# Down projection: the second product of one token pair and the first of the next as one run, the seventh product in a bank of its own

## The chip, the cores and the metric

The kernel runs on one core of one Trainium2 chip. A core has a matrix engine (TensorE, PE in the profile; its weight loads are listed apart as PEld), VectorE (DVE), ScalarE (ACT), GpSimd (POOL) and a queue engine, SyncE (SP), which issues nearly all transfers of this kernel. The engines run side by side and wait for one another by semaphores. Each engine, and SP's queue of transfers too, works in the order in which its instructions were written; what waits holds all that stands behind it. Matrix products are summed in PSUM, eight banks of 128 x 512 float32. The metric is the device time of one execution in microseconds (us); the middle of several executions is compared.

## The reference

One transformer block on 2048 tokens of width 1024: layer norm with scale and shift from a condition, linear attention, a gated residual, a second layer norm, and a gated feed-forward part of width 3584 with its own gated residual.

```python
x = x + ga * _A_ref(h, A_wqkv, A_wo)
h = _layernorm(x, axis=-1) * (1 + cb) + sb
x = x + gb * (_gelu(h @ w_gate) * (h @ w_up) @ w_down)
```

The change touches only the last product, `y @ w_down`, with y of 2048 x 3584, and what follows it: the multiplication by `gb` and the addition of x.

## The kernel before

The down projection takes the tokens in eight pairs of 128-token blocks. For one pair the product is a 2 x 2 block product: two token blocks by two halves of the 3584-wide contraction (even and odd blocks of 128) times two halves of the contraction by two halves of the 1024 output columns. It is done with seven products in place of eight (Strassen's scheme in Winograd's form). Each product is 14 matmuls of 128 x 128 by 128 x 512, one per block index j.

- Products 1 and 2 take y and the weights as they are, in bfloat16 (tiles `ya`, `wd`).
- Products 5, 6, 7, 3 and 4 take sums of y blocks (S0 to S4, tile `sb`, written by `d_s`) and differences of weight blocks (tiles `dt` and `dh`, written by `d_t`), in fp32r, a float32 format. The profile calls them f32.

Product 5 uses S0, 6 uses S1, 7 uses S2, 3 uses S3 and 4 uses S4. S0, S2 and S4 share one buffer and S1 and S3 another, and the two change roles with each pair. So S2 can be written only when product 5 has read S0, and so on. Each sum is two DVE instructions of 896 columns, S4 two ScalarE copies. S0 needs both the even and the odd blocks of the pair.

A pair has four PSUM banks, b0 to b0 + 3; pairs alternate between banks 0 to 3 and 4 to 7. The order before was 1, 5, 6, 2, 7, 3, 4. Product 1 starts bank b0, and ScalarE copies it to bank b0 + 2 (`d_cp`), where products 6, 7 and 4 are added one after another. Product 5 starts bank b0 + 3 and is copied to an SBUF tile `de` (`d_ecp`). `d_add` adds `de` to bank b0 + 2 and writes bank b0 + 1 after product 6, and bank b0 + 3 after product 7. Product 2 is added in bank b0, product 3 in bank b0 + 1. As each of the four output parts is whole, `evac` multiplies it by the gate row (L1576), adds the x part `xq` (L1577) and stores it (L1578). Its DVE instructions stand in the one DVE queue, its store in SP's.

SP's queue carries, for each pair, two loads of y, even and odd blocks (`y_in`, L1571, 896 KB each), four loads of x parts (`x_in`, L1568, 128 KB each) and four stores (L1578). Each `ya` buffer is single: the even blocks of the next pair can be loaded when product 1 and S2 are done with the old ones, the odd blocks when product 2 and S4 are. An `x_in` waits until the store that read the same `xq` buffer has landed. All orders in this part are those of the program text; the planner that reorders an earlier stretch of the kernel does not reach it.

Pair 0 is cut in two: products over the first eight j by the seven-product scheme, the rest by plain products (`down`, L1593), in `d_pair0`. Two of its output parts (1 and 2) are evacuated only during pair 1, by a hook that `d_pair` calls after each product. During pair 1 DVE also makes the last weight differences (`d_t`, L1621). In the last pair DVE multiplies three weight differences by the gate row (`t_gb`, L1652). Product 3 of that pair is cut in two there: eight j with `evac_part` behind them, and after product 4 the other six in a bank of their own, whose sum (`evac_sum`, L1685) is the last DVE work of the kernel.

All products of this part are issued by `d_prod` (L1672).

Of the kernel before, what the change touches and what calls it, by code (L numbers as in the profile page):

```python
# [330 lines left out]
def bass_adaLN_cond__linear_attn_block__geglu_ffn__prompt_kernel(  # L331
# [18 lines left out]
    with ExitStack() as es:  # L350
# [201 lines left out]
        sch = Sched()  # L552
        T, A, V, G, Q = PE_, ACT_, DVE_, POOL_, SP_
# [588 lines left out]
        for c_ in range(10, NCH):  # L1142
            b = seq.index(("k", c_ // 2 * 2, 0)) - (9 if c_ % 2 else 12)
# [422 lines left out]
        def x_in(i, *ns):  # L1566
            for n in ns:
                sch.dma(Q, lambda e, n=n: e.dma_start(XQ[n][:], scr_x[:, 2 * i + n // 2, n % 2 * 512:n % 2 * 512 + 512]), wr=r_xq(n), deps=[x_st[i // 2]], note=f"xq{i}.{n}")  # L1568
# [5 lines left out]
        def evac(c_, k, b, c0, c1):  # L1574
            n = 2 * (c_ % 2) + k
            sch.op(V, lambda e: e.tensor_tensor(PS(b), PS(b), GBB[:, c0:c1], ALU.mult), prd=pr(b), pwr=pr(b), rd=R_GBB, note=f"x2a c{c_}.{k}")  # L1576
            sch.op(V, lambda e: e.tensor_tensor(XQ[n][:, :], PS(b), XQ[n][:, :], ALU.add), prd=pr(b), rd=r_xq(n), wr=r_xq(n), note=f"x2b c{c_}.{k}")  # L1577
            sch.dma(Q, lambda e: e.dma_start(out_v[:, c_, c0:c1], XQ[n][:, :]), rd=r_xq(n), note=f"out{c_}.{k}")  # L1578
# [29 lines left out]
        def d_t(i, q):  # L1608
            j0, j1 = 0, 2
            w = WDT[q][:, 2 * j0:2 * j1, :].rearrange("p (j r) d -> p j r d", r=2)  # L1610
            b = lambda r, cc: (w[:, :, r, cc * 512:(cc + 1) * 512], r_wh(q, r, cc, f"wd{q}", j0, j1))
            t32 = lambda k: (dt_ap(q, k, j0, j1)[0].bitcast(f32), dt_ap(q, k, j0, j1)[1])
            dst, wr = dt_ap(q, i, j0, j1)
            if i == 3:
                src, rd = b(1, 1)
                sch.op(A, lambda e: e.activation(dst, src, ACTF.Copy), rd=rd, wr=wr, note=f"dtcp {q}")
                return
            (in0, r0), (in1, r1) = ((b(0, 1), b(0, 0)), (b(1, 1), t32(0)), (b(1, 1), b(0, 1)), None, (b(1, 0), t32(1)))[i]
            if i == 4:
                in0, in1 = (t_.rearrange("p j (h c) -> p j h c", h=2) for t_ in (in0, in1))  # L1620
            sch.op(V, lambda e: e.tensor_tensor(dst, in0, in1, ALU.subtract), rd=r0 + r1, wr=wr, note=f"dtsum {q}.{i}")  # L1621
# [13 lines left out]
        def d_s(ca, i, hs=(0, 1)):  # L1635
            cb, n = ca + 1, nj(ca)
            for j0, j1 in (((0, min(n, NSJ)), (NSJ, n))[h] for h in hs):
                if j0 >= j1:
                    continue
                dst, wr = ds_ap(ca, i, j0, j1)  # L1640
                if i == 4:
                    src, rd = y_ap(cb, 1, j0, j1)
                    sch.op(A, lambda e, dst=dst, src=src: e.activation(dst, src, ACTF.Copy), rd=rd, wr=wr, note=f"dscp {cb}")  # L1643
                    continue
                s_ = lambda k: (ds_ap(ca, k, j0, j1)[0].bitcast(f32), ds_ap(ca, k, j0, j1)[1])
                (in0, r0), (in1, r1), op = ((y_ap(cb, 0, j0, j1), y_ap(cb, 1, j0, j1), ALU.add), (s_(0), y_ap(ca, 0, j0, j1), ALU.subtract),
                                            (y_ap(ca, 0, j0, j1), y_ap(cb, 0, j0, j1), ALU.subtract), (y_ap(ca, 1, j0, j1), s_(1), ALU.subtract))[i]
                sch.op(V, lambda e, dst=dst, in0=in0, in1=in1, op=op: e.tensor_tensor(dst, in0, in1, op), rd=r0 + r1, wr=wr, note=f"dssum{i} {cb}")  # L1648

        def t_gb(q):  # L1650
            t_, r_ = dt_ap(q, 3, 0, 2)
            sch.op(V, lambda e: e.tensor_tensor(t_, t_.bitcast(f32), GBB[:, 512:1024].unsqueeze(1).to_broadcast([P, 2, 512]), ALU.mult), rd=r_ + R_GBB, wr=r_,  # L1652
                   note=f"dtsum gb{q}")

        def d_prod(ca, b0, k, own=None, js=None):
            b = b0 + {1: 0, 2: 0, 5: 3, 6: 2, 7: 2, 4: 2, 3: 1}[k] if own is None else own
            i = {1: None, 2: None, 5: 0, 6: 1, 7: 2, 3: 3, 4: 4}[k]
            o = None
            js = range(nj(ca)) if js is None else js
            for j in js:  # L1660
                q, jj = divmod(j, 2)
                dst = PS(b)
                if i is None:
                    l_, rl = y_ap(ca, k - 1, j, j + 1)
                    r_, rr = WDT[q][:, 2 * jj + k - 1, 0:512], r_wh(q, k - 1, 0, f"wd{q}", jj, jj + 1)
                else:
                    l_, rl = ds_ap(ca, i, j, j + 1)
                    t_, rr = dt_ap(q, i, jj, jj + 1)
                    r_ = t_[:, 0]
                    if i == 4:  # L1670
                        dst = dst.rearrange("p (h c) -> p h c", h=2)
                o = sch.op(T, lambda e, l_=l_, r_=r_, j=j, dst=dst: e.matmul(dst, l_[:, 0, :], r_, start=(k in (1, 5) or own is not None) and j == js[0], stop=j == js[-1], skip_group_check=True),  # L1672
                           rd=rl + rr, pwr=(pr(b) if j == js[0] else ()), note=f"down P{k} c{ca} j{j}", overwrite_ok=True)
            pset_writer(b, o)

# [15 lines left out]
        def d_cp(dst, src, note):  # L1691
            sch.op(A, lambda e: e.activation(PS(dst), PS(src), ACTF.Copy), prd=pr(src), pwr=pr(dst), note=note)

        def d_add(dst, src):
            sch.op(V, lambda e: e.tensor_tensor(PS(dst), PS(src), DE[:, :], ALU.add), prd=pr(src), rd=R_DE, pwr=pr(dst), note="dpadd")

        def d_ecp(b):
            sch.op(A, lambda e: e.activation(DE[:, :], PS(b), ACTF.Copy), prd=pr(b), wr=R_DE, note="descp")
# [5 lines left out]
        def d_pair0(hook):  # L1704
            parts = parts_of(0)
            for k in (2, 6, 5, 0, 7, 3, 13, 11, 12, 4):
# [12 lines left out]
                    d_add(3, 2)  # L1719
                hook(k)  # L1720

        def d_pair(i, hook):
            ca, b0 = 2 * i, i % 2 * 4
            last = i == 2 * CPG - 1
            parts = parts_of(i)

            def y_next(r):
                if not last:
                    y_in(i + 1, r)

            for k in (1, 5, 6, 2, 7, 3, 4):
                if last and k == 3:
                    d_prod(ca, b0, 3, None, range(6, NDJ))
                    evac_part(*parts[1])
                    continue
                d_prod(ca, b0, k)
                if k == 1:
                    d_cp(b0 + 2, b0, "dpcp")
                elif k == 5:
                    d_ecp(b0 + 3)  # L1740
                    d_s(ca, 2)
                elif k == 6:
                    d_add(b0 + 1, b0 + 2)
                    d_s(ca, 3)
                    y_next(0)
                elif k == 2:
                    evac(*parts[0])
                elif k == 7:
                    d_add(b0 + 3, b0 + 2)
                    d_s(ca, 4)  # L1750
                    y_next(1)
                    evac(*parts[3])
                elif k == 3:
                    evac(*parts[1])
                    d_s(ca + 2, 0)
                else:
                    if not last:
                        d_s(ca + 2, 1)
                    evac(*parts[2])
                    if last:  # L1760
                        d_prod(ca, b0, 3, 0, range(6))
                        evac_sum(*parts[1][:2], 0, *parts[1][3:])
                hook(k)
# [62 lines left out]
        for n in range(12):  # L1826
            q, i = divmod(n, 4)
# [56 lines left out]
        def hooks(i):  # L1884
            def hook(k):
                more = i + 1 < 2 * CPG
                if i == 1:
                    if k == 1:
                        d_t(2, 5)
                        d_t(2, 6)  # L1890
                    if k in (6, 2, 7):
                        d_t(4, {6: 4, 2: 5, 7: 6}[k])
                    if k in (6, 7):
                        n = 1 if k == 6 else 2
                        evac(*parts_of(0)[n])
                        x_in(1, n)
                else:
                    if k == 1:
                        x_in(i, 0, 3, 1)
                    elif k == 5:  # L1900
                        x_in(i, 2)
                    if not more and k in (5, 6):
                        for q in {5: (0, 1), 6: (2,)}[k]:
                            t_gb(q)
            return hook

        d_pair0(hook0)
        for i in range(1, 2 * CPG):
            d_pair(i, hooks(i))

# [74 lines left out]
```

## Time and profile before

| | us |
|---|---|
| three runs | 782.47, 782.76, 783.43 |
| median | 782.76 |
| span of the profiled execution (first to last instruction) | 780.9 |
| PE / DVE / ACT busy in the span | 770.2 / 645.9 / 374.6 |
| down projection, first to last matmul | 598.6 to 778.0 |
| granted TensorE clock, whole span | 1.00 |

The profile is one execution. Its own device time is not recorded beside the span; the median of the runs is 1.9 above the span, which is what lies before the first and behind the last instruction. A row of the timeline shows the start, the length, the engine and line, what is written and read, how many like instructions were merged into the row, and in brackets how long the engine had been idle and what ended that. "SPq" rows are SP issuing transfers; their length is that of issuing, not of the transfer. Merged SP rows include the waits between the issues. When the text says that a load landed so many us after its issue, the landing is the one that the trace holds for that transfer.

### The profile page before, as it was taken

The page shows a single profiled execution, that of the slowest core. Times are in us where ns is not written, and L with a number is a line of the kernel's source. Part 1 is how long each engine was busy: PE and PEld are TensorE (multiplying, and loading weights), DVE is VectorE, ACT ScalarE, POOL GpSimd, SP SyncE. Part 2 cuts the span into 40 slices and gives each one's busy share as a digit, 9 for nine tenths or more (in the row PEclk, how much of TensorE's full clock was granted, in tenths as well). Part 3 has the DMA queues.
Part 4 walks back from the last instruction along what each step waited for, and adds up shares of the span by engine and source line. Part 5 has one row for each costly group of instructions (what it writes and reads, how often), then busy time and mean ns, then how long its engine had stood idle before and what let it go on. Part 6 is the DMA issues. An engine that isn't in the chain of part 4 may idle for free.

```text
span 780.9 us, 10753 instructions
## 1 busy us (share of the span) xinstructions
PE 770.2 (99%) x3825; PEld 496.2 (64%) x3883; DVE 645.9 (83%) x964; ACT 374.6 (48%) x629; POOL 47.5 (6%) x126
## 2 busy tenths in 40 slices
PE   8999999999999999999999999999999999999998
PEld 4444445666445667667676767667676576677766
DVE  6699988897899878787989888888989888676767
ACT  2497743242466487878755555555555211111111
POOL 2031300000321011100000000000000000000000
PEclk9999999999999999999999999999999999999999
DMA  9879749939999358867353865535356334443331
GB/s 284 256 167 252 158 91 215 255 80 196 203 287 231 82 138 212 230 175 215 99 145 108 250 211 172 148 96 161 97 147 221 111 127 139 144 141 114 126 125 60
DMA packets 196940, 130.22 MB, mean 167 GB/s; under 512 B 69516, under 2 KB 182420, under 8 KB 195864
## 3 DMA queue, kind: packets, MB, share of 16 engines
q1 hardware_dynamic: 196872, 129.55, 62.4%
q8 instruction: 30, 0.49, 0.3%
q14 instruction: 22, 0.18, 0.1%
q10 hardware_dynamic: 16, 0.00, 0.0%
HBM read 92.55 MB, written 23.35 MB: 148 GB/s over the span
## 4 chain that ended last, share of the span: by engine, by line
PE 95%; SPq 2%; DMA 1%; DVE 1%; issue 1%; ACT 0%; DVEq 0%; ACTq 0%
PE ps_all L1458 45%; PE ps_all L1672 21%; PE ps_all L895 7%; PE ps_all L934 7%; PE ps_all L1283 7%; PE ps_all L880 5%; PE ps_all L1593 1%; SPq L598 1%; DMA wmq<-in_w_mod_dram 1%; SPq L603 1%; DMA h1T<-xh 0%; PE ps_all L913 0%; PE ps_all L1201 0%; PE ps_all L1240 0%; DVE h1T L724 0%
## 5 line engine op out<-in xcount | busy, mean ns | idle before, releaser
L1458 PE MATMUL ps_all<-ss,tp 128*128 128x512 f32 x896 | 214.3, 396 | 0.0
L1458 PEld LDWEIGHTS ps_all<-ss,tp 128*128 128x128 f32 x896 | 168.3, 188 | 37.8 <-DVE ss L1413 0.2
L1672 PE MATMUL ps_all<-dt,sb 128*128 128x512 f32 x424 | 102.5, 398 | 0.0
L1481 ACT ACTIVATE ge<-ps_all 128x512 f32<-128x512 f32 x112 | 64.1, 597 | 73.8 <-DVE ps_all L1469 62.1
L1458 PE MATMUL ps_all<-h2a,wt 128*128 128x512 bf16 x421 | 95.7, 379 | 1.8
L1672 PEld LDWEIGHTS ps_all<-dt,sb 128*128 128x128 f32 x424 | 79.6, 188 | 18.5 <-DVE sb L1648 0.3
L1476 DVE TENSOR_TENSOR ps_all<-ps_all,es 128x512 f32<-128x512 f32 x54 | 37.6, 699 | 49.4 <-ACT es L1466 49.0
L1488 DVE TENSOR_TENSOR ys<-ge,ps_all 128x512 bf16<-128x512 f32 x112 | 74.4, 684 | 3.8 <-PE ps_all L1672 0.5
L1458 PEld LDWEIGHTS ps_all<-h2a,wt 128*128 128x128 bf16 x448 | 38.0, 98 | 57.3 <-ACT ps_all L1463 16.9
L1433 DVE TENSOR_TENSOR tp<-wt 128x1024 fp32r<-128x1024 bf16 x56 | 68.1, 1217 | 1.8 <-DMA wt<-in_B_w_up_dram 1.8
L1433 DVE TENSOR_TENSOR tp<-wt,tp 128x1024 fp32r<-128x1024 bf16 x56 | 68.2, 1218 | 0.0
L934 PE MATMUL ps_all<-h1T,wq 128*128 128x512 bf16 x256 | 56.7, 379 | 0.0
L880 PE MATMUL ps_all<-wk,h1T 128*128 128x512 bf16 x239 | 55.3, 379 | 1.1 <-DMA wk<-in_A_wqkv_dram 0.5
L1283 PE MATMUL ps_all<-w,pq 128*128 128x512 bf16 x249 | 55.7, 379 | 0.5 <-issue 0.2
L1458 PE MATMUL ps_all<-ar,tp 128*128 128x512 f32 x224 | 55.5, 390 | 0.0
L869 ACT ACTIVATE eb<-ps_all 128x512 f32<-128x512 f32 x64 | 36.3, 594 | 37.6 <-PE ps_all L880 16.0
L1672 PE MATMUL ps_all<-wd,ya 128*128 128x512 bf16 x199 | 47.5, 380 | 0.7
L1458 PEld LDWEIGHTS ps_all<-ar,tp 128*128 128x128 f32 x224 | 42.1, 188 | 8.9
L1463 ACT ACTIVATE ps_all<-ps_all 128x512 f32<-128x512 f32 x56 | 32.6, 582 | 26.8 <-PE ps_all L1458 26.5
L934 PEld LDWEIGHTS ps_all<-h1T,wq 128*128 128x128 bf16 x256 | 25.0, 98 | 30.0
L1283 PEld LDWEIGHTS ps_all<-w,pq 128*128 128x128 bf16 x256 | 24.6, 98 | 30.3 <-issue 1.1
L1643 ACT ACTIVATE sb<-ya 128x896 fp32r<-128x896 bf16 (+1 forms) x16 | 14.5, 913 | 58.8 <-PE ps_all L1672 58.8
(141 smaller groups left out, 976.3 us busy)
## 6 DMA issues: line engine op xcount, KB each, us to landing
wt<-in_B_w_gate_dram SPq DMA_DIRECT2D x28, 512.0 KB, 4.0
wt<-in_B_w_up_dram SPq DMA_DIRECT2D x28, 512.0 KB, 5.2
scr_y<-ys SPq DMA_DIRECT2D x28, 512.0 KB, 3.2
ya<-scr_y SPq DMA_DIRECT2D x14, 896.0 KB, 4.9
rb<-scr_rd SPq DMA_DIRECT2D x32, 256.0 KB, 6.0
wd<-in_B_w_down_dram SPq DMA_DIRECT2D x7, 1024.0 KB, 7.6
wmst<-in_w_mod_dram SPq DMA_DIRECT2D x6, 1024.0 KB, 6.2
wmq<-in_w_mod_dram SPq DMA_DIRECT2D x8, 512.0 KB, 7.5
```

The costliest lines, as they stand in the source:

```text
L869: sch.op(A, lambda e: e.activation(EB[i][:, :], PS(bank), ACTF.Exp), prd=pr(bank), wr=rng, note=f"{note}.exp")
L880: o = sch.op(T, lambda e, dc=dc: e.matmul(PS(bank), H1[sg][:, ci, dc, :], W_[:, dc, jg * 512:(jg + 1) * 512], start=(dc == 0), stop=(dc == ...
L895: o = sch.op(T, lambda e, c_=c_: e.matmul(PS(bank, 0, n), PK[c_][:, g * P:(g + 1) * P], xrow(c_, o_, o_ + n), start=(c_ == 0), stop=(c_ == ...
L934: o = sch.op(T, lambda e, dc=dc: e.matmul(PS(b), WQ[:, dc, qc * P:(qc + 1) * P], H1[sg][:, :, dc, :], start=(dc == 0), stop=(dc == NDC - 1 ...
L1283: last[half] = sch.op(T, lambda e, g=g, half=half: e.matmul(PS(b0 + half), PQ[sg][:, g, ci * P:(ci + 1) * P], W2[:, g, half * 512:(half + ...
L1433: sch.op(V, lambda e: e.tensor_tensor(TP[k][:], in0, in1 if k in (0, 2) else in1[:], ALU.subtract), rd=r0 + r1, wr=r_tp(k), deps=[x1_ops[7 ...
L1458: o = sch.op(T, lambda e, l_=l_, r_=r_, dc=dc: e.matmul(PS(b), l_, r_, start=fresh and dc == 0, stop=dc == ND2 - 1, skip_group_check=True) ...
L1463: sch.op(A, lambda e: e.activation(PS(BB + t), PS(BA + t), ACTF.Copy), prd=pr(BA + t), pwr=pr(BB + t), note="pcp")
L1476: sch.op(V, lambda e: e.tensor_tensor(PS(BC + t), PS(BC + t), ES[t][:, :], ALU.add), prd=pr(BC + t), rd=r_2k(OFF_ES[t], f"es{t}"), pwr=pr( ...
L1481: sch.op(A, lambda e: e.activation(GE[i][:, :], PS(b), ACTF.Gelu_apprx_tanh), prd=pr(b), wr=r_2k(OFF_GE[i], f"ge{i}"), note="gelu")
L1488: sch.op(V, lambda e: e.tensor_tensor(YS[s_][:, 2 * h:2 * h + 2, t, :], q(GE[i][:, :]), q(PS(b + 1)), ALU.mult), rd=r_2k(OFF_GE[i], f"ge{i ...
L1672: o = sch.op(T, lambda e, l_=l_, r_=r_, j=j, dst=dst: e.matmul(dst, l_[:, 0, :], r_, start=(k in (1, 5) or own is not None) and j == js[0] ...
```

## The change

The order of the products in a pair becomes 5, 6, 7, 2, then product 1 of the next pair, then 3 and 4. Product 1 of pair 1 is issued ahead, behind pair 0. So product 2 of one pair and product 1 of the next stand next to one another, both in bfloat16.

Product 7 no longer adds to bank b0 + 2. For pairs 1 to 7 it starts bank b0 + 3, which product 5 has left by then. A new function `d_join` has ScalarE copy it to `de`, and DVE adds `de` to bank b0 + 1 (result to bank b0 + 3) and to bank b0 + 2. Pair 0 keeps its form.

What stood behind the moved products moves along: the load of the next pair's odd blocks (`y_next(1)`) from behind product 7 to behind product 2, and the evacuation of part 3 stays behind product 7. The hooks are spread anew. In pair 1 the weight differences and the evacuation of pair 0's part 2 stand behind products 6, 7 and 2. The x loads of a pair stand behind product 1 (part 3) and product 4 (part 0) of the pair before, and behind its own product 5 (parts 1 and 2). The three scalings of the last pair stand behind products 7 (two) and 2 (one), where they stood behind 5 and 6.

```diff
-            b = b0 + {1: 0, 2: 0, 5: 3, 6: 2, 7: 2, 4: 2, 3: 1}[k] if own is None else own
+            b = b0 + {1: 0, 2: 0, 5: 3, 6: 2, 7: 3 if ca else 2, 4: 2, 3: 1}[k] if own is None else own
...
-start=(k in (1, 5) or own is not None) and j == js[0]
+start=(k in (1, 5) or k == 7 and ca > 0 or own is not None) and j == js[0]
...
+        def d_join(b0):
+            d_ecp(b0 + 3)
+            d_add(b0 + 3, b0 + 1)
+            d_add(b0 + 2, b0 + 2)
+
+        def d_open(i):
+            b = i % 2 * 4
+            d_prod(2 * i, b, 1)
+            d_cp(b + 2, b, "dpcp")
...
-            for k in (1, 5, 6, 2, 7, 3, 4):
+            for k in (5, 6, 7, 2, 1, 3, 4):
+                if last and k == 1:
+                    continue
...
+                if k == 1:
+                    d_open(i + 1)
+                    hook(k)
+                    continue
                 d_prod(ca, b0, k)
-                if k == 1:
-                    d_cp(b0 + 2, b0, "dpcp")
-                elif k == 5:
+                if k == 5:
                     d_ecp(b0 + 3)
                     d_s(ca, 2)
                 elif k == 6:
                     d_add(b0 + 1, b0 + 2)
                     d_s(ca, 3)
                     y_next(0)
+                elif k == 7:
+                    d_join(b0)
+                    d_s(ca, 4)
+                    evac(*parts[3])
                 elif k == 2:
+                    y_next(1)
                     evac(*parts[0])
-                elif k == 7:
-                    d_add(b0 + 3, b0 + 2)
-                    d_s(ca, 4)
-                    y_next(1)
-                    evac(*parts[3])
...
                 if i == 1:
-                    if k == 1:
-                        d_t(2, 5)
-                        d_t(2, 6)
-                    if k in (6, 2, 7):
-                        d_t(4, {6: 4, 2: 5, 7: 6}[k])
+                    if k in (6, 7, 2):
+                        d_t(4, {6: 4, 7: 5, 2: 6}[k])
                     if k in (6, 7):
                         n = 1 if k == 6 else 2
                         evac(*parts_of(0)[n])
                         x_in(1, n)
                 else:
-                    if k == 1:
-                        x_in(i, 0, 3, 1)
-                    elif k == 5:
-                        x_in(i, 2)
-                    if not more and k in (5, 6):
-                        for q in {5: (0, 1), 6: (2,)}[k]:
+                    if k == 5:
+                        x_in(i, 1, 2)
+                    if not more and k in (7, 2):
+                        for q in {7: (0, 1), 2: (2,)}[k]:
                             t_gb(q)
+                if more and k in (1, 4):
+                    x_in(i + 1, 3 if k == 1 else 0)
...
         d_pair0(hook0)
+        d_open(1)
+        d_t(2, 5)
+        d_t(2, 6)
         for i in range(1, 2 * CPG):
             d_pair(i, hooks(i))
```

More of the change, by code (lines that the diff above doesn't have):

```diff
@@ L1671, in d_prod @@
                         dst = dst.rearrange("p (h c) -> p h c", h=2)
-                o = sch.op(T, lambda e, l_=l_, r_=r_, j=j, dst=dst: e.matmul(dst, l_[:, 0, :], r_, start=(k in (1, 5) or own is not None) and j == js[0], stop=j == js[-1], skip_group_check=True),
+                o = sch.op(T, lambda e, l_=l_, r_=r_, j=j, dst=dst: e.matmul(dst, l_[:, 0, :], r_, start=(k in (1, 5) or k == 7 and ca > 0 or own is not None) and j == js[0], stop=j == js[-1], skip_group_check=True),
                            rd=rl + rr, pwr=(pr(b) if j == js[0] else ()), note=f"down P{k} c{ca} j{j}", overwrite_ok=True)
```

## The prediction

> **What bounds the kernel now.** I read the page's busy line and its chain of work first. The chain says which engine sets the end.
>
> ```profile
> PE 770.2 (99%) x3825; PEld 496.2 (64%) x3883; DVE 645.9 (83%) x964; ACT 374.6 (48%) x629; POOL 47.5 (6%) x126
> ...
> PE 95%; SPq 2%; DMA 1%; DVE 1%; issue 1%; ACT 0%; DVEq 0%; ACTq 0%
> ```
>
> TensorE (PE) is busy nearly everywhere and is 95% of the chain. So an edit pays only if it shortens PE's own stream, and costs only if it makes PE wait or lengthens what follows its last matmul. The change touches the down projection alone, so I read the timeline of one steady pair there (start, length, both in us).
>
> ```profile
> 686.65 0.70 DVE L1576 TENSOR_TENSOR ps_all<-ps_all,gbb 128x512 f32<-128x512 f32 x1 [0.94 <-PE ps_all L1672]
> ...
> 689.49 2.09 DVE L1648 TENSOR_TENSOR sb<-ya,ya 128x896 fp32r<-128x896 bf16 x2 [1.34 <-DMA ya<-scr_y]
> 689.62 2.71 PEld L1672 LDWEIGHTS ps_all<-wd,ya 128*128 128x128 bf16 x14 [0.26 <-issue]
> ...
> 692.44 6.35 PEld L1672 LDWEIGHTS ps_all<-dt,sb 128*128 128x128 f32 x28
> ...
> 711.66 2.71 PEld L1672 LDWEIGHTS ps_all<-wd,ya 128*128 128x128 bf16 x14 [0.26 <-issue]
> ```
>
> Two pairs' first products start 711.66 - 689.62 = 22.04 apart. The f32 loads step by (6.35 - 0.19) / 27 = 0.228; longer undisturbed runs give 0.2267. The bf16 matmuls step by 0.216. Without any seam a pair is 70 x 0.2267 + 28 x 0.216 = 21.92, so the two bf16 runs cost 0.12 together: **0.06 per run**. The 0.26 of idle printed at each run's start is the weight loader's, and most of it lies under matmuls that still stream.
>
> Third, the stretch where the first two pairs overlap, since DVE is fullest there (18.1 of the 20 us from 640 to 660), with SyncE's (SP's) queue.
>
> ```profile
> 640.17 0.32 SPq L1568 DMA_DIRECT2D xq<-scr_x  x1
> 640.54 0.43 SPq L1578 DMA_DIRECT2D out_dram<-xq  x1
> ...
> 641.08 0.36 SPq L1571 DMA_DIRECT2D ya<-scr_y  x1
> ...
> 643.06 2.92 SPq L1578 DMA_DIRECT2D out_dram<-xq  x2
> ...
> 647.06 2.09 DVE L1648 TENSOR_TENSOR sb<-ya,ya 128x896 fp32r<-128x896 bf16 x2
> 647.77 0.33 SPq L1568 DMA_DIRECT2D xq<-scr_x  x1
> ...
> 648.36 1.79 PEld L1672 LDWEIGHTS ps_all<-dt,sb 128*128 128x128 f32 x8
> ```
>
> The load at 641.08 brings the odd blocks of pair 2. The sum S0 made from it starts at 647.06, and pair 2's fifth product, its first user, at 648.36: there is only 0.2 to spare once S0's first half (1.09) is made. The xq load at 647.77 is issued behind an output (the second of the two from 643.06, at 645.65) whose landing it waits for, 2.1 later. Such a wait holds all of SP's queue.
>
> Last, the end.
>
> ```profile
> 776.20 1.32 PEld L1672 LDWEIGHTS ps_all<-dt,sb 128*128 128x128 f32 x6
> ...
> 776.62 0.70 DVE L1576 TENSOR_TENSOR ps_all<-ps_all,gbb 128x512 f32<-128x512 f32 x1 [1.36 <-PE ps_all L1672]
> 777.43 0.69 DVE L1577 TENSOR_TENSOR xq<-ps_all,xq 128x512 bf16<-128x512 f32 x1
> 778.03 0.68 DVE L1685 TENSOR_TENSOR xq<-ps_all,de 128x512 bf16<-128x512 f32 x1
> 778.74 0.33 SPq L1686 DMA_DIRECT2D out_dram<-xq  x1
> ```
>
> DVE idles 1.36 before the last three operations: it keeps up with PE, and the last sum starts 1.83 after the last six loads do.
>
> **The change part by part.** *Fewer bf16 runs.* Pairs 1 to 7 have two each, 14. After it there are 8: one for pair 1's first product, six merged, one second product in the last pair. Six fewer by 0.06 is **-0.4**. Matmul counts do not change. By the printed idle it would be 6 x 0.26 = 1.6; I take 0.4, since the pair's pitch already contains all that a run costs.
>
> *Seventh product in its own bank.* Per pair this adds a ScalarE copy (0.60, the row of the fifth product's copy) and one DVE add (0.61 pitch, 0.70 long). In a steady pair, counted from its fifth product's start, the seventh ends near 10.0, the copy at 10.6, the adds at 11.9, the evacuation of part 3 at 13.4 and of part 0 at 14.8. DVE then idles until the third product ends at 19.2. Bank 1 is wanted by the third product only at 15.6, and bank 2 by the fourth at 18.8. So this costs nothing, hidden by DVE's idle time; without that cover it would be at most 0.6 a pair.
>
> *S0 of the next pair.* The fifth product now follows the fourth directly. After the third product's end at 19.24: evacuation 1.42, first half 1.09, done at 21.8; the fifth starts at 21.98. It just fits. S2, wanted by the seventh at 6.35, has its first half by 5.2. The range here is 0 to 0.1 a pair; I take 0.
>
> *The even-block load, steady.* The next pair's first product moves up to 12.56. Its load stands in SP behind part 2's output (issued near 4.2), two xq loads and a third that waits for that output's landing (1.7 to 2.1), so it is issued near 6.7. The full ya loads of this stage whose landing the trace holds took 4.5 to 6.05 from issue (over all 18 ya loads the median is 4.8, the longest 7.3): it lands at 11.2 to 12.75. I take nothing; the upper end is 0.25 in each of six pairs, 1.5.
>
> *The odd-block load of pair 2.* This is the costly step. It moves from behind the seventh product to behind the second, which in pair 1 puts it past the output of pair 0's part 2 and the xq load that waits for that output's landing. DVE after the evacuation of pair 0's part 1 (its last row starts at 637.68, 0.6 to the next): from 638.28 two adds 1.21, part 3 of pair 1 1.41, one weight difference 1.13, pair 0's part 2 1.49, to 643.5. Output issued at 643.6, xq load 1.8 to 2.1 behind it (both gaps stand in SP's rows: 638.39 to 640.17, 645.65 to 647.77), the ya load 0.4 later, near 645.9; landing 4.8 later, 650.7; S0's first half 0.1 + 1.09 with 0.05 to PE: 651.9. PE without the wait would be there at 648.3. So PE waits **3.6**, by the ends (4.5 after the shorter gap, 6.05 after the longer) 3.2 to 5.1. Behind this wait on DVE stand S0's second half, S1 and part 2's evacuation; S1 is ready at 654 against its product's start at 655, so nothing more is late. The wait occurs once: from pair 2 on no foreign output stands before that load, it leaves near 13.9 and lands by 18.8 (20 with the slowest landing), against 20.6.
>
> *The tail.* The last pair's three scalings of weight differences by the gate row (1.22 each, pitch 1.135) move from behind the fifth and sixth products to behind the seventh and second. DVE from the copy's end at 10.7: adds 1.21, part 3 1.40, two scalings 2.27, part 0 1.40, the third 1.135, the partial evacuation 1.39, part 2 1.40: the last sum starts at 20.9. The last six matmuls' loads start at 17.6, so the sum starts 3.3 after them instead of 1.83: **+1.45**, between 1.2 and 1.7 by the spread of pitches. The third scaling ends at 18.2, its first user starts at 18.5: no wait there.
>
> *Sum:* -0.4 + 3.6 + 1.45 = **+4.65**. The profiled execution's span of 780.9 becomes 785.6. The median of 782.76 stands 1.9 above that span (launch and end around it, taken as unchanged): **787.4**, 0.6% slower.
>
> [...] The trace's longest PE idle is 2.2 us, at the very start, and the granted clock reads 1.00 in every window. A wait of 3.6 has no row. [...] I sum at full clock.
>
> **The rivals.**
> *The clock drops in the wait.* [...] For it: the idle is longer than any in the trace. Against: the clock of 1.00 after 2.2 idle. Chance 0.10.
>
> *Every pair waits for its even blocks.* If those loads take 6.05, as the four behind xq loads at 655, 675, 697 did or nearly did, six waits of 0.25 come on top: 788.9. Against: only one xq load is fresh before them now. Chance 0.10.
>
> *The odd-block load is not late.* If the change doesn't hold it back (its landing by 647), only runs and tail remain: 782.76 - 0.4 + 1.45 = 783.8, within 0.2%. Against: SP's rows issue strictly in order and show that very wait. Chance 0.07.
>
> *The other side: a seam costs far more than the pitch says.* Place: the six removed runs. To end over 0.2% faster (1.57) against 3.6 + 1.45, each must be worth over 1.1. The pitch gives 0.06, the printed idle 0.26, so only a cost in the rows' blind spots could do it, for instance 1.2 each: 780.6. Chance 0.03.
>
> **How the numbers follow.** My forecast has 0.70, with 786.8 to 789.2 as its own range (3.2 + 1.2 - 0.4 to 5.1 + 1.7 - 0.4 on 782.76). The overall range is 785.6 to 789.8: its lower end is the forecast's lower end with 0.26 instead of 0.06 for each of the six runs, its upper end takes in most of the two dearer rivals, and what is left out are the two cheap rivals and about 0.07 above. A change of 0.2% (1.6 us) is about what a measurement of this kernel can tell from none. Slower: 0.70 + 0.10 + 0.10 = 0.90; within: 0.07; faster: 0.03.
>
> **What would show it.** In the profile after: the fifth product of pair 2 waits over 3 us for DVE's S0, which waits for a ya load issued near 646, behind an xq load; eight bf16 starts with 0.26 of loader idle, six of them 28 loads long; pairs about 21.98 apart; DVE without idle from the last seventh product to the last sum, which starts over 3 behind the last six loads; a granted clock of 1.00 around 652. I am wrong if the ya load of pair 2 is issued by 642, if the six middle pairs grow above 22.04, or if the last sum still starts within 2 of the last loads.

## The result and the profile after

The changed kernel takes 789.35 us (median of five executions; 788.86 to 790.96) against 782.76 before. The ratio is 1.0089, with a 95% interval of 1.0077 to 1.0100: 0.9% slower. The profiled execution took 790.67; its span is 788.9, 8.0 above the 780.9 of before.

First the page: the chain of work by engine, and the row of the granted TensorE clock over 40 slices.

```profile
PEclk9999999999999999999999999999999998999999
...
PE 93%; DMA 3%; DVE 2%; SPq 2%; issue 0%; DVEq 0%; ACT 0%; ACTq 0%
```

PE has 93% of the chain instead of 95, and transfers and DVE have gained. One slice of the clock row, from about 651 to 671, has an 8. The view of waits names what PE waited for, total, times and longest:

```profile
PE ps_all L1672 <- DVE sb L1648: 3.4, 1, 3.4
...
PE ps_all L1672 <- DMA ya<-scr_y: 0.3, 1, 0.3
```

Both are new, and both are in the down projection. The timeline where pairs 1 and 2 meet shows the first, SP's queue ahead of the rest:

```profile
641.16 2.92 SPq L1578 DMA_DIRECT2D out_dram<-xq  x2
645.48 0.33 SPq L1568 DMA_DIRECT2D xq<-scr_x  x1
645.92 0.37 SPq L1571 DMA_DIRECT2D ya<-scr_y  x1
...
645.34 3.13 PEld L1672 LDWEIGHTS ps_all<-dh,sb 128*128 128x128 f32 x14
...
646.92 0.69 DVE L1577 TENSOR_TENSOR xq<-ps_all,xq 128x512 bf16<-128x512 f32 x1
651.16 2.09 DVE L1648 TENSOR_TENSOR sb<-ya,ya 128x896 fp32r<-128x896 bf16 x2 [3.55 <-DMA ya<-scr_y]
...
652.31 9.70 PEld L1672 LDWEIGHTS ps_all<-dt,sb 128*128 128x128 f32 x32 [3.84 <-DVE sb L1648]
```

The load of pair 2's odd blocks is issued at 645.92 (641.08 before), behind the x load at 645.48, which waited for the landing of the second store in the row above (issued at 643.75). It lands at 651.07. DVE idles 3.55, makes S0, and the fifth product starts at 652.31. Its predecessor's 14 loads started at 645.34, so it was due 14 x 0.2267 later, at 648.51: PE lost **3.8**.

The windows (busy time and number of instructions of each engine, then granted clock, transfer share and GB/s) show what the wait set off:

```profile
648.00:650.00 2.00, 0.90 (x4) 0.39 (x3) 0.00 (x0) 0.00 (x0) 0.00 (x0) 1.00 0.92 346
650.00:652.00 2.00, 0.00 (x0) 0.00 (x0) 0.83 (x1) 0.00 (x0) 0.00 (x0) 0.74 0.60 210
652.00:654.00 2.00, 1.69 (x4) 1.40 (x5) 2.00 (x3) 0.00 (x0) 0.00 (x0) 0.50 0.00 0
...
656.00:658.00 2.00, 2.00 (x7) 1.58 (x6) 1.66 (x2) 0.00 (x0) 0.00 (x0) 0.55 0.18 61
658.00:660.00 2.00, 2.00 (x10) 1.61 (x9) 1.09 (x1) 0.60 (x1) 0.00 (x0) 1.00 0.65 178
```

The clock is halved from about 650.96 (0.74 over 2 us is half speed for 1.04) to 657.8, 6.8 us. Six or seven f32 matmuls fall in 2 us there, ten after it: by their starts they step by 0.427 instead of 0.227. Twelve of them do, which is **2.4** more.

The steady pairs are as short as forecast, by the loads:

```profile
686.51 5.73 PEld L1672 LDWEIGHTS ps_all<-wd,ya 128*128 128x128 bf16 x28 [0.26 <-issue]
692.35 3.17 PEld L1672 LDWEIGHTS ps_all<-dt,sb 128*128 128x128 f32 x14
...
708.48 3.57 PEld L1672 LDWEIGHTS ps_all<-wd,ya 128*128 128x128 bf16 x18 [0.26 <-issue]
```

One bf16 run of 28 loads per pair, and 708.48 - 686.51 = 21.97 per pair, 0.067 less than before. One pair is longer:

```profile
724.94 0.34 SPq L1578 DMA_DIRECT2D out_dram<-xq  x1
725.37 3.84 SPq L1568 DMA_DIRECT2D xq<-scr_x  x3
...
729.31 0.37 SPq L1571 DMA_DIRECT2D ya<-scr_y  x1
730.45 2.70 PEld L1672 LDWEIGHTS ps_all<-wd,ya 128*128 128x128 bf16 x14 [0.26 <-issue]
...
733.91 2.70 PEld L1672 LDWEIGHTS ps_all<-wd,ya 128*128 128x128 bf16 x14 [0.75 <-DMA ya<-scr_y]
```

The store at 724.94 took 3.9 to land, the third x load waited for it and held the even-block load until 729.31. The first product of the next pair, due 14 x 0.216 behind 730.45, came 0.43 late. Last the tail:

```profile
782.68 1.32 PEld L1672 LDWEIGHTS ps_all<-dt,sb 128*128 128x128 f32 x6
...
784.55 0.69 DVE L1576 TENSOR_TENSOR ps_all<-ps_all,gbb 128x512 f32<-128x512 f32 x1
785.34 0.69 DVE L1577 TENSOR_TENSOR xq<-ps_all,xq 128x512 bf16<-128x512 f32 x1
785.95 0.68 DVE L1685 TENSOR_TENSOR xq<-ps_all,de 128x512 bf16<-128x512 f32 x1
```

DVE has no idle left (1.36 before), and the last sum starts 3.27 behind the last six loads, where it was 1.83.

| where the 8.0 of the profiled execution lie | us |
|---|---|
| the down projection begins later (598.73 for 598.56, ahead of all that changed) | +0.2 |
| wait of pair 2's fifth product | +3.8 |
| half clock behind it | +2.4 |
| wait for even blocks near 733 | +0.4 |
| tail | +1.4 |
| six bf16 runs fewer | -0.4 |
| sum | +7.8 |

### The profile page after: what moved, and what is told of

Same layout as the page of the kernel before. It is cut to its first block, busy times and chain, and to the rows that moved or that the text cites. A ratio compares the mean times of both kernels' runs of the same rounds, so it can differ in the third digit from the quotient of the medians.

```text
span 788.9 us, 10827 instructions
## 1 busy us (share of the span) xinstructions
PE 776.8 (98%) x3883; PEld 498.4 (63%) x3883; DVE 648.1 (82%) x971; ACT 377.0 (48%) x636; POOL 47.4 (6%) x126
## 4 chain that ended last, share of the span: by engine, by line
PE 93%; DMA 3%; DVE 2%; SPq 2%; issue 0%; DVEq 0%; ACT 0%; ACTq 0%
PE ps_all L1458 45%; PE ps_all L1672 18%; PE ps_all L895 7%; PE ps_all L1283 7%; PE ps_all L934 7%; PE ps_all L880 6%; PE ps_all L1593 1%; DMA ya<-scr_y 1%; DMA wmq<-in_w_mod_dram 1%; SPq L598 1%; SPq L603 1%; PE ps_all L913 0%; DVE xq L1577 0%; DVE dt L1652 0%; DVE ps_all L1576 0%; DVE ps_all L1695 0%
## 5 line engine op out<-in xcount | busy, mean ns | idle before, releaser
L1458 PE MATMUL ps_all<-h2a,wt 128*128 128x512 bf16 x448 | 101.6, 380 | 0.0
L1672 PEld LDWEIGHTS ps_all<-dt,sb 128*128 128x128 f32 x424 | 81.4, 192 | 22.2 <-DVE sb L1648 4.1
L1698 ACT ACTIVATE de<-ps_all 128x512 f32<-128x512 f32 x15 | 9.0, 597 | 103.6 <-PE ps_all L1672 103.6
```

The source lines that it names most:

```text
L1458: o = sch.op(T, lambda e, l_=l_, r_=r_, dc=dc: e.matmul(PS(b), l_, r_, start=fresh and dc == 0, stop=dc == ND2 - 1, skip_group_check=True) ...
```

## The experiments

My theory was that one load, held back in SP's queue, causes the wait in pair 2, that this wait halves the clock, and that the scalings cause the tail. The rivals were DVE's own load in pair 1, a clock that falls for another reason, and a price of the added copy and add in every pair. In the first four runs the kernel before had 782.68, in the last four 782.87.

### Pair 0's part 2 behind product 2

```diff
-                    if k in (6, 7):
+                    if k in (6, 2):
                         n = 1 if k == 6 else 2
                         evac(*parts_of(0)[n])
                         x_in(1, n)
```

> The changed kernel, with the evacuation of pair 0's part 2 and the x load that waits for its store moved from behind product 7 to behind product 2 of pair 1, so that the load of pair 2's odd blocks no longer stands behind them. Nothing is left out. Theory (queue order makes that load late): it is issued near 641.6 instead of 645.9 and lands by 647; the wait of pair 2's fifth product falls from 3.8 us to 0.2 or less, the granted clock stays 1.00, and 3.6 plus the 0.6 to 2.4 of half-clock time go: 783 to 785. Rival (the wait comes from DVE's load in pair 1, not from the queue): the wait stays above 2 us, since DVE does the same work in that stretch.

Measured: 784.25 (783.54 to 785.5), 1.0020 of before (1.0011 to 1.0030). The timeline:

```profile
641.16 0.36 SPq L1571 DMA_DIRECT2D ya<-scr_y  x1
...
648.21 3.97 PEld L1672 LDWEIGHTS ps_all<-dt,sb 128*128 128x128 f32 x18 [0.19 <-DVE sb L1648]
```

The load is issued 4.8 earlier (the whole stretch lies 0.4 earlier in this trace), and the loader's idle before the fifth product falls from 3.84 to 0.19. DVE does the same work in that stretch, so its load was not the cause. The granted clock is between 0.998 and 1.00 in all ten executions, against 0.995 to 0.997 in the changed kernel's five. About 5 of the 6.6 are gone by moving two DVE instructions and two transfers. What is left of the loss, 1.6, is about the tail, which this run leaves as it was.

### Only the x load moved

```diff
                     if k in (6, 7):
                         n = 1 if k == 6 else 2
                         evac(*parts_of(0)[n])
-                        x_in(1, n)
+                    if k in (6, 2):
+                        x_in(1, 1 if k == 6 else 2)
```

> The changed kernel, with only the x load of pair 1's part 2 moved behind product 2; the store of pair 0's part 2 stays ahead of the load of pair 2's odd blocks. Theory: the load is issued near 644.1 (1.8 earlier, the landing of the store that the x load waited for), lands near 649, and the fifth product waits 1.5 to 2.0 instead of 3.8. By the clock theory, an idle of PE below 2 us leaves the granted clock at 1.00: 784.9 to 786. Rival (any wait here drops the clock): the clock falls below 1.00 behind this wait as well, and the time is 1 to 2.5 higher.

Measured: 785.44 (784.95 to 787.11). The timeline:

```profile
643.15 0.38 SPq L1571 DMA_DIRECT2D ya<-scr_y  x1
...
649.47 2.61 PEld L1672 LDWEIGHTS ps_all<-dt,sb 128*128 128x128 f32 x12 [2.02 <-DVE sb L1648]
```

The wait is 2.0 in place of 3.8 (the load is issued 2.8 earlier, but the whole stretch lies 1.0 earlier in this trace): the part of it that the x load's wait for a landing had caused is gone, the part that the store ahead caused is left. In five of six executions the clock stays at 0.999 or 1.00; in the profiled one (0.999) PE itself idled 1.6. The slowest, 787.11, shows 0.997 and has no trace. So the theory's forecast for the clock held in five of six.

### The wait filled with matmuls

```diff
+                if i == 1 and k == 4:
+                    d_fill(14, 3)
```

`d_fill(n, b)` issues n matmuls of `wd` by `wd` into bank b.

> The changed kernel, with 14 plain bf16 matmuls of no use (about 3.0 us) put between the fourth product of pair 1 and the fifth of pair 2, in a bank that the fifth product starts anew. They fill the wait and change no load, no DVE work and no queue of transfers. Theory (the clock fell because PE idled): S0 comes at the same moment as in the changed kernel and the fifth product starts as late, but the granted clock stays 1.00 and its matmuls step by 0.23, so the time is 787 to 788.4, with less spread than 788.9 to 791.0. Rival (the clock falls for another reason, such as the load that lands then): matmuls behind it step by 0.43 still, 789 to 791.

Measured: 787.67 (787.28 to 789.3), clock 0.999 or 1.00 in all four. Timeline and windows:

```profile
652.41 3.73 PEld L1672 LDWEIGHTS ps_all<-dt,sb 128*128 128x128 f32 x17 [0.82 <-DVE sb L1648]
```

```profile
653.00:655.00 2.00, 2.00 (x10) 1.67 (x9) 2.00 (x3) 0.00 (x0) 0.00 (x0) 1.00 0.00 0
```

The fifth product starts at 652.41 as against 652.31, so the late load is untouched. But ten matmuls fall in 2 us behind it where the changed kernel had six or seven. So it was PE's idling that halved the clock (3.4 in the changed kernel, 0.3 here): the loads, DVE's work and the queues were the same. The forecast of less spread did not hold (2.0 against 2.1). The execution of 789.3 is the profiled one: there the even-block load of pair 3 took 7.45 to land (issued 659.06), and PE waited for it 1.3.

### The scalings earlier

```diff
-                    if not more and k in (7, 2):
-                        for q in {7: (0, 1), 2: (2,)}[k]:
-                            t_gb(q)
+                    if not more and k in (5, 6, 2):
+                        t_gb({5: 0, 6: 1, 2: 2}[k])
```

> The changed kernel, with the three scalings of the last pair's weight differences behind products 5, 6 and 2 (one each) instead of 7, 7 and 2. Theory (they lengthen the tail by standing on DVE between the last seventh product and the last sum): the last sum starts 1.85 to 1.95 behind the loads of the last six matmuls instead of 3.27, and the time falls by 1.35 to 787.5 to 789.6 (the wait in pair 2 and the clock's spread stay). Rival (the tail is set by the last stores or by the other added DVE work): the distance stays above 2.8 and the time does not move.

Measured: 788.80 (787.3 to 790.63). The tail in the timeline:

```profile
782.01 1.32 PEld L1672 LDWEIGHTS ps_all<-dt,sb 128*128 128x128 f32 x6
...
782.43 0.70 DVE L1576 TENSOR_TENSOR ps_all<-ps_all,gbb 128x512 f32<-128x512 f32 x1 [0.46 <-PE ps_all L1672]
...
783.85 0.68 DVE L1685 TENSOR_TENSOR xq<-ps_all,de 128x512 bf16<-128x512 f32 x1
```

The last sum starts 1.84 behind the last loads, as before the change, and DVE waits for PE again. So the tail of 1.43 is the scalings' place. The median fell by 0.55 only, where 1.35 was forecast. The half clock behind pair 2's wait is still there (0.996 or 0.997), and the four executions spread by 3.3, so the time alone could not have shown the tail's share. What spreads them is not shown: 788.57 and 790.63 have the same clock of 0.996.

### Fewer matmuls in the wait

```diff
-                    d_fill(14, 3)
+                    d_fill(4, 3)
```

> The changed kernel with 4 useless bf16 matmuls (0.9 us) in the wait of pair 2 instead of 14, so that PE idles about 2.5 to 2.8. Theory (the clock falls by how much PE did in fixed stretches of 3.41 us, since both half-clock times seen lasted 6.83 = 2 x 3.41): it falls in some executions and not in others, by where the wait lies in the stretch; times of 787.3 to 790.5, granted clock from 0.995 to 1.00. Rival (only an idle of 3.41 or more lets it fall): the clock stays at 0.999 or 1.00 in every execution, 787.3 to 788.3.

Measured: 788.40. The four executions, time and granted clock: 786.73 and 788.02 at 0.999, 788.78 and 789.33 at 0.997. One of them lies below the range of the theory. The profiled one is that of 788.02:

```profile
652.63 1.46 PEld L1672 LDWEIGHTS ps_all<-dt,sb 128*128 128x128 f32 x7 [2.98 <-DVE sb L1648]
```

PE itself idled 2.5 there, and the clock stayed at 1.00 in the windows over the wait. In two others the granted clock is lower, but they have no trace, so how long PE idled in them is not known.

The traces at hand tell more of the theory. In the profile of the changed kernel the time from one change of the clock to the next is 189 times 3.413 us at full clock, 2 times at half and 38 times at full; in that of the kernel before it is 227 times at full clock. The last change is a fall behind the last matmul, where it costs nothing. Steps of 3.413 counted back from it give stretches for the other traces too; that the clock could have changed only at their borders is the author's estimate from these counts. Here is PE's busy time (the second number) in the stretches that hold the wait: two of the changed kernel, one of this run, one of the run that moved only the x load.

```profile
647.55:650.96 3.41, 1.35 (x6) 0.77 (x5) 0.06 (x1) 0.00 (x0) 0.00 (x0) 1.00 0.89 320
650.96:654.37 3.41, 2.06 (x5) 1.68 (x6) 3.21 (x4) 0.00 (x0) 0.00 (x0) 0.50 0.09 31
...
648.33:651.75 3.42, 1.82 (x9) 0.75 (x7) 0.26 (x1) 0.00 (x0) 0.00 (x0) 1.00 0.91 338
...
648.05:651.46 3.41, 1.99 (x9) 1.65 (x10) 3.14 (x4) 0.00 (x0) 0.00 (x0) 1.00 0.22 75
```

The clock fell at the end of the stretch with PE busy for 1.35, and not behind those with 1.82 and 1.99. The run with earlier scalings fell behind 1.33. At the kernel's end it fell behind 1.29 (in the first run of the next section) and not behind 1.86 (in the run with pair 0's part 2 moved). In the changed kernel the stretch with 2.06 of busy time at half clock was followed by another at half clock, and that one, with PE busy for all of its 3.42, by full clock. The border counted so cuts this run's idle of 2.5 into 1.6 and 0.9, and the clock fell behind neither part. The rival, which asks for an idle of 3.41, is refuted by the changed kernel's own trace, where the clock fell 2.1 into the idle, and by the run with earlier scalings, where the whole idle was 3.33. The ends of matmuls are modelled in a profile, so the busy times are rough.

### All three mended

```diff
-                    if k in (6, 7):
+                    if k in (6, 2):
                         n = 1 if k == 6 else 2
                         evac(*parts_of(0)[n])
                         x_in(1, n)
...
-                    if k == 5:
+                    if k == 6:
                         x_in(i, 1, 2)
...
-                    if not more and k in (7, 2):
-                        for q in {7: (0, 1), 2: (2,)}[k]:
-                            t_gb(q)
+                    if not more and k in (5, 6, 2):
+                        t_gb({5: 0, 6: 1, 2: 2}[k])
```

> The changed kernel with three moves and nothing left out: pair 0's part 2 and its x load behind product 2 of pair 1; the three scalings behind products 5, 6 and 2; the x loads of a pair's parts 1 and 2 behind product 6, after the load of the next pair's even blocks. Theory (all of the loss is late loads, the half-clock time that the largest of them causes, and the scalings): pair 2's fifth product waits 0.3 at most, no first product waits for its even blocks, the last sum starts under 2 behind the last loads, and what remains is the gain of six runs of 0.06: 782.1 to 783.0 against about 782.7 before. Rival (the added copy and add for the seventh product, or the order itself, cost something in every pair): pairs are longer than 22.04 and the time stays above 783.5.

Measured: 782.63 (782.10 to 783.15), 0.9996 of before (0.9987 to 1.0005). A second version adds further moves in the order of DVE and SP:

```diff
             elif k == 12:
                 ...
                 evac(*parts_of(0)[3])
+                evac(*parts_of(0)[1])
+                x_in(1, 1)
...
-                    if k in (6, 2):
-                        n = 1 if k == 6 else 2
-                        evac(*parts_of(0)[n])
-                        x_in(1, n)
+                    if k == 6:
+                        evac(*parts_of(0)[2])
+                        x_in(1, 2)
...
                 elif k == 7:
                     d_join(b0)
                     d_s(ca, 4)
-                    evac(*parts[3])
                 elif k == 2:
                     y_next(1)
+                    evac(*parts[3])
                     evac(*parts[0])
```

> As the run before, with three more moves: pair 0's part 1 is evacuated before pair 1 starts, its part 2 behind product 6, and the evacuation of part 3 of every pair stands behind product 2, after the load of the odd blocks, so that this load is issued at product 2's end (near 639.5 for pair 2 instead of 641.2). Theory: also the last 0.3 of wait in pair 2 goes; pairs of 21.97 throughout: 781.9 to 782.6, by 0.0 to 0.1% faster than before. Rival (late evacuation of part 3 holds up the fifth product or DVE): waits of PE for DVE appear in every pair, above 783.

Measured: 782.35 (781.74 to 783.52), 0.9995 of before (0.9986 to 1.0003). Two neighbouring pairs in its timeline:

```profile
680.02 5.73 PEld L1672 LDWEIGHTS ps_all<-wd,ya 128*128 128x128 bf16 x28 [0.26 <-issue]
...
701.99 2.06 PEld L1672 LDWEIGHTS ps_all<-wd,ya 128*128 128x128 bf16 x11 [0.26 <-issue]
```

Both are back at the time of before and not distinguishable from it. In both profiles the view of waits shows none of PE in the down projection, and the steady pairs take 21.97. So neither the seventh product's own bank, its copy and its add, nor the new order costs anything that can be seen. The whole loss came from what had been moved along. What the merged runs bring is to be seen in the traces alone: from the first load of the down projection to the last six it is 177.24 in the second version (598.52 to 775.76) and 177.64 before (598.56 to 776.20). This 0.4 is 0.05% and below what these comparisons resolve (their intervals are about 0.09% to each side). No version beats the kernel before clearly.

### More runs in the kernel before

```diff
+                if k == 6:
+                    d_prod(ca, b0, 2, None, range(7))
-                d_prod(ca, b0, k)
+                d_prod(ca, b0, k, None, range(7, NDJ) if k == 2 else None)
```

> The kernel before, with product 2 of pairs 1 to 7 cut in two halves of seven matmuls, one before product 6 and one behind it, so that there are seven more bf16 runs. Nothing is left out. Theory (a run costs 0.06, as the pairs' pitch says): pairs of 22.10 to 22.11 instead of 22.04, 0.45 more in all, 783.0 to 783.4. Rival (a run costs the idle of 0.26 that the rows print): pairs of 22.30, 1.8 more, 784.4 to 784.8.

Measured: 784.30 (783.87 to 786.55), 1.0022 of before (1.0013 to 1.0031). My forecast of the time missed, and by the time alone the rival would be nearly right. The timeline decides otherwise:

```profile
691.05 2.71 PEld L1672 LDWEIGHTS ps_all<-wd,ya 128*128 128x128 bf16 x14 [0.26 <-issue]
...
697.31 1.19 PEld L1672 LDWEIGHTS ps_all<-wd,ya 128*128 128x128 bf16 x7 [0.26 <-issue]
...
702.05 1.19 PEld L1672 LDWEIGHTS ps_all<-wd,ya 128*128 128x128 bf16 x7 [0.26 <-issue]
...
713.13 0.76 PEld L1672 LDWEIGHTS ps_all<-wd,ya 128*128 128x128 bf16 x5 [0.26 <-issue]
```

Every run prints its 0.26 of idle, yet a steady pair takes 22.073 by the unrounded starts, 0.034 more than before for one run more. Seven of these are 0.24. The rest of the 1.6 in the spans (782.5 against 780.9) is not the price of runs as such: the down projection begins 0.27 later, pair 1 is 0.95 longer (with a wait of PE of 0.6 for a DVE add, in the stretch where DVE is full) and pair 2 0.18 longer. The printed idle is refuted as the price of a run. My own 0.06 is not a constant either: 0.034 for cutting a run in two halves, 0.067 for merging two whole ones.

## Why the prediction was right or wrong

The direction and the overall range (785.6 to 789.8) held the median of 789.35, though two of the five executions, 790.67 and 790.96, lie above it. The predicted 787.4 was 2 too low, and the forecast's own range of 786.8 to 789.2 missed it by 0.15. So the overall range held because it took in the dearer rivals, not because the sum was right. In the profiled execution the span grew by 8.0 where the sum had 4.65; 2.4 of the difference is the half clock.

- *Fewer bf16 runs, -0.4.* Right: 0.067 per pair in the pitch.
- *The seventh product's bank, 0; S0 of the next pair, 0.* Right. Steady pairs run at 21.97 without a wait for DVE.
- *The odd-block load of pair 2, +3.6.* Right in mechanism and nearly in size: issued at 645.92 as forecast for 645.9, landed at 651.07 for 650.7, wait 3.8. The two moves of the x load and of the store divide it: about 1.8 for the landing that the x load waits for, 1.8 for the store's own turn, 0.2 left by the loader's idle.
- *The tail, +1.45.* Right: 1.44 (3.27 for 1.83), and undone by moving the scalings back.
- *The even-block load, 0.* Half right. The forecast set against it a wait of 0.25 in all six pairs. What came was a wait in a single pair: 0.43 in the changed kernel, 1.3 in the profiled execution of the filled one, 0.6 in that of the run with pair 0's part 2 moved (first product at 749.44, its load issued at 742.47 landing after 6.93), when a store or a load landed about 2 later than usual. The step lacked the rare slow landing that the queue passes on. Of the loads that it names, three (655.20, 675.20, 697.42) took 6.02 to 6.05, one took 5.02, and one has no landing in the trace.
- *"I sum at full clock."* This is the step that failed: the half-clock time behind the wait was put at nothing, and it was 2.4 in the profiled execution. The reason given was an idle of 2.2 at the very start that left the clock at 1.00. That was a misreading of the trace before. The views print 1.00 where they hold no record of the clock, and the first record of that trace begins at 6.14. The timeline of the kernel before shows what ran ahead of it and behind it:

```profile
4.82 0.15 PEld L949 LDWEIGHTS ps_all<-warm 128*128 128x128 bf16 x1 [0.28 <-issue]
...
5.25 0.15 PEld L949 LDWEIGHTS ps_all<-warm 128*128 128x128 bf16 x1 [0.28 <-issue]
...
7.06 1.46 PE L949 MATMUL ps_all<-warm 128*128 128x512 bf16 x6
```

Each load belongs to a bf16 matmul of 128 x 512. Up to 6.10 they start 0.43 apart, the step of pair 2's half clock; from 7.06 six such matmuls take 1.46 together, a step of 0.216. So TensorE ran at half rate behind that idle, and the kernel before already held a row for it. (How long PE had idled ahead of the first instruction is not in the trace.)

The rival that the clock drops in the wait, which had only a chance of 0.10, names what happened. No run shows the size that the overall range, up to 789.8, allows for it; what the runs showed in its place is half clock for 6.8 us (650.96 to 657.8, 2 x 3.41), in which twelve matmuls step by 0.427 instead of 0.227, 2.4 in all. The clock fell 2.1 after PE's last matmul had ended (648.89 to 650.96), within an idle of 3.42, and PE had been busy for 1.35 of the 3.41 before the fall.

Between the changed kernel's five executions the clock goes with the time: 788.86 to 789.35 at a granted clock of 0.997, 790.67 and 790.96 at 0.995. In the profiled one, 790.67, the half clock behind the last matmul (787.49 to the end) is in that figure too and costs nothing. By an estimate from these figures, 3.41 fewer at half speed would save 1.7, and the times differ by 1.3 to 2.1; but the executions at 0.997 have no trace, so this is not shown.

## What to carry to other kernels

When products are reordered, follow each transfer that is issued between them past every other entry of its queue; here the products' new order was free, and a load that came to stand behind a store and a wait for its landing cost 3.8, though no instruction was added to it. Price a wait of the matrix engine beyond its own length: here an idle of 3.4 was followed by half clock that cost 2.4 in the profiled execution, and one of 2.5 (four filling matmuls) by none. Read the price of a seam from the pitch of whole repeats, not from the idle printed before an instruction, and look at the last few microseconds of the vector engine's queue before moving work towards the end.

## What the runs showed of the hardware

- Between the recorded changes of the granted clock lie 189, 2 and 38 times 3.413 us in the trace of the changed kernel and 227 times in that of the kernel before. Of the stretches of 3.41 counted back from the last change, the clock fell behind those with PE busy for 1.29, 1.33 and 1.35 and stayed behind those with 1.82, 1.86 and 1.99. The trace of the changed kernel and that of the run with earlier scalings both show half clock for 6.8 us (650.96 to 657.8, and 650.4 to 657.3), with six or seven f32 matmuls of 128 x 512 in 2 us instead of ten; in the changed kernel they step by 0.427 instead of 0.227. Useless matmuls in the idle time kept the clock at 0.999 or 1.00 and gained 1.7 in the median.
- A store of 128 KB with no load of y just ahead of it landed in 1.7 to 2.4 in the steady pairs of the kernels before and after, but one took 3.9 in the changed kernel (issued 724.94). (Stores right behind such a load took 3.8 to 5.1.) Loads of 896 KB took 4.5 to 6.1 in these two kernels, but one took 7.45 in the filled run (issued 659.06) and one 6.93 in the run with pair 0's part 2 moved (issued 742.47). In all three cases the trace has a 16 KB transfer of the instruction queue at the same time (726.1, lasting 1.6; 661.5, lasting 2.6; 744.6, lasting 1.8; others of that queue in the down projections of these three runs last 0.9 to 1.4). That these are the cause was not tested.
- The weight loader's idle of 0.26 before each change from f32 to bf16 is almost wholly hidden: in a steady pair, a cut of a run into two costs PE 0.034.
